# A fused gated-linear-attention and SoLU kernel: weighted keys of the later groups turned by VectorE squares and SBUF transfers in place of array transposes

## The chip, the cores and the metric

The kernel runs on one core of a Trainium2 chip. The metric is the device time of one execution in microseconds (us), as the median of several runs. A core has five engines with their own instruction queues: TensorE (PE in the profile, with its weight loads listed apart as PEld), VectorE (DVE), ScalarE (ACT), GpSimd (POOL) and SyncE (SP). SP issues nearly all DMA transfers here. Each engine works through its queue in program order.

## The reference, cut to what matters

For each of 4 batches and 8 heads of width 48 a state matrix runs over 768 time steps; its output, with the heads side by side, is the input of a layer with a softmax-weighted activation and a layer norm.

```python
for t in range(S):                                     # S = 768, D = 48
    state = alpha[:, :, t, :, None] * state + einsum('bhd,bhe->bhde', k[:, :, t], v[:, :, t])
    y[:, :, t] = einsum('bhd,bhde->bhe', q[:, :, t], state)
x = y.transpose(0, 2, 1, 3).reshape(3072, 384)
h = x @ w_in                                           # 384 -> 1024
solu = h * softmax(h)
ln = (solu - mean(solu)) / sqrt(var(solu) + 1e-6) * g_ln
out = ln @ w_out                                       # 1024 -> 384
```

## The kernel before, in words

Time is cut into six groups of 128 steps (G = 6, P = 128). Within a group the recurrence is written as a masked product: the queries are multiplied by the running products of alpha, the keys by their inverse counterpart (the "weighted keys" kT), and the scores are kT times queries. What came in earlier groups enters through `state`, which is read with the same weighted queries. After a group, `next_state` adds the product of the weighted keys and the values to the state.

**Layout.** A head has 48 features, stored as 32 and 16. The weighted keys `kT` are a tile of 128 x 12 x 128 (features of four batches in four quarters of 32 partitions; twelve blocks j: eight with 32 features of one head each, four with 16 features of two heads each; 128 time steps). `next_state` (L333) needs the same keys with time in the partitions. That is the tile `kg`. `keys_back` (L284) makes it: twelve transposes of 128x128 by PE (L287) into three PSUM banks, and three copies by ScalarE (L289). `next_state` then issues 96 small products (L342), and VectorE adds them to the state (L351).

**Preparing a group.** `keys_T` and `keys`: VectorE transposes of k (L184, L187), then GpSimd's product with the scan (L233). `scan_on` (L216): forward scans of alpha on VectorE. `lasts` (L186) and `firsts` (L183): VectorE transposes of q into `qe` and `qv`. `queries(i)` (L241): GpSimd multiplies them by the scan (L244). `apart` (L235): two ScalarE multiplications (L237) that spread `qe` into the second half of `qv`. `scores` (L262): 64 PE products per half (L268), which read kT and qv. `masked` (L276): VectorE (L279). `read_state` and `read_values`: PE (L300).

**The second part, by group.** `up(g, s)` for s from 0 to 7: six PE products (L366), then e = exp(h) on ScalarE (L380), u = h·e on VectorE (L381), u² on ScalarE (L382). `running(g, s)` (L385) adds e on GpSimd and u² on VectorE to running sums p (both L397). `down(n, half)`: eight PE products for one batch of the group before (L477). `finish(n)` (L482), after both halves: three tiny VectorE operations (L495 to L500), a power on GpSimd (L508), a scaling on ScalarE into `o_sb` (L510), and a store issued by SP (L511).

**The order.** It is written by hand: a manual schedule, in which program order is the order of each queue. The loop from L858 has a round g for each group of the second part, and prepares group g + 1 within it. Each round has eight steps s, and a plan of four tables says what of the preparation goes where: `head` before `up`, `behind` after `up` and after `finish`, `middle` ahead of `down`, `tail` after it. Round 1 uses the plan `first`, round 2 `second`, rounds 3 and 4 `usual`; in round 5 no group is left to prepare. `finish` comes in steps 2, 4 and 6 and after the round.

```python
for s in range(FC):
    at("head", s)
    up(g, s)
    if after is not None:
        finish(after)
    at("behind", s)
    if rise and s:
        running(g, s)
    at("middle", s)
    down(n, half)
    at("tail", s)
```

In `second` the queries are made in step 3, `apart` comes in step 4 and the first scores at the tail of step 5. In `usual` the three stand in steps 2, 3 and 4.

Of the kernel before, what the change touches and what calls it, by code (L numbers as in the profile page):

```python
# [9 lines left out]
FP = mybir.dt.float32  # L10
# [6 lines left out]
P = 128  # L17
# [15 lines left out]
def fast_path(ctx, tc, q, k, v, alpha, moe_w_in, moe_w_out, moe_g_ln, out):  # L33
# [12 lines left out]
    nc = tc.nc  # L46
    B, H, S, D = q.shape
# [5 lines left out]
    NB = H + NP  # L53
# [8 lines left out]
    def pool(name, bufs, **kw):  # L62
        return ctx.enter_context(tc.tile_pool(name=name, bufs=bufs, **kw))

    const = pool("const", 1)
    two = pool("two", 4)
# [32 lines left out]
    TQ = P // 32  # L99
# [21 lines left out]
    kT = const.tile([P, NB, P], FP, name="kT")  # L121
    kg = const.tile([P, NB, P], FP, name="kg")
# [6 lines left out]
    def load(src, dst, g):  # L129
        t = slice(g * P, (g + 1) * P)  # L130
        for b in range(B):
            nc.sync.dma_start(
                out=dst[32 * b : 32 * b + 32].rearrange("t h u d -> t h (u d)"),
                in_=src[b, :, t, :].rearrange("h (t u) d -> t h (u d)", u=TQ),
            )
# [31 lines left out]
    def load_v(g):  # L167
        t = slice(g * P, (g + 1) * P)
        for dst, src in ((slice(0, E0), slice(0, E0)), (slice(48, 64), slice(E0, D))):
            nc.sync.dma_start(  # L170
                out=vn[:, :, :, dst].rearrange("p b h d -> p (b h) d"),
                in_=v[:, :, t, src].rearrange("b h p d -> p (b h) d"),
            )
# [9 lines left out]
    def firsts(src, dst):  # L183
        nc.vector.transpose(out=dst.rearrange("p h (t u) -> p h u t", u=TQ), in_=src[:, :, :, 0:E0])  # L184

    def lasts(src, dst):  # L186
        nc.vector.transpose(  # L187
            out=dst.rearrange("p j (i t u) -> p u j i t", u=TQ, i=2),
            in_=src[:, :, :, E0:D].rearrange("p (j i) u d -> p u j i d", i=2),
        )  # L190

    def alpha_T(g):
        nc.gpsimd.memset(aT[:, :, 0:1], 0.0)
        firsts(an, aT[:, 0:H, 1:SW])
        lasts(an, aT[:, H:NB, 1:SW])
# [20 lines left out]
    def scan_on(g, i):  # L216
        part = slice(NP * i, NP * i + NP)
        s = seed[i % 2]
        if i == 2:
            nc.vector.tensor_copy(out=fend[:, g], in_=h4[:, :, 1])  # L220

        least = small.tile([P, NP, 1], FP, name="least")
        nc.vector.tensor_scalar(out=least, in0=h4[:, part, 1:2], scalar1=LEAST, scalar2=None, op0=ALU.max)  # L223
        nc.vector.reciprocal(out=s[:, :, 0:1], in_=least)
        scan(aT[:, part], aT[:, part], s, False)

    def keys_T(g):
        firsts(kn, kT[:, 0:H])
        lasts(kn, kT[:, H:NB])

    def keys(g):
        for part in (slice(0, H), slice(H, NB)):
            nc.gpsimd.tensor_tensor(out=kT[:, part], in0=kT[:, part], in1=hk[:, part], op=ALU.mult)  # L233

    def apart():  # L235
        for i in range(2):
            nc.scalar.mul(  # L237
                out=qv[:, H : 2 * H].rearrange("p (j i) t -> p j i t", i=2)[:, :, i], in_=qe, mul=parity[:, i : i + 1]
            )

    def queries(i):  # L241
        part = slice(NP * i, NP * i + NP)
        q = qe if i == 2 else qv[:, part]
        nc.gpsimd.tensor_tensor(out=q, in0=q, in1=aT[:, part, 1:SW], op=ALU.mult)  # L244

    def decay(g):

        if g == 0:
            return
        s = state[:, 0:H, 0:64]  # L250
        nc.gpsimd.tensor_tensor(out=s, in0=s, in1=h4[:, 0:H, 1:2].to_broadcast([P, H, 64]), op=ALU.mult)
        for i in range(2):
            s = state[:, H : 2 * H, 0:64].rearrange("p (j i) e -> p j i e", i=2)[:, :, i]
            nc.gpsimd.tensor_tensor(out=s, in0=s, in1=h4[:, H:NB, 1:2].to_broadcast([P, NP, 64]), op=ALU.mult)

    def quarter(b):
        return slice(32 * b, 32 * b + 32)

    def banks(name, shape, n=B):
        return [ps_a.tile([P] + shape, FP, tag=f"a{b}", name=f"{name}{b}") for b in range(n)]  # L260

    def scores(g, half, a=None):  # L262
        a = a or banks("a", [NP, P])
        for i in range(NP):
            h = half * NP + i
            for kb, qb in ((h, h), (H + h // 2, H + h)):
                for b in range(B):
                    nc.tensor.matmul(  # L268
                        a[b][:, i], lhsT=kT[quarter(b), kb], rhs=qv[quarter(b), qb], start=kb == h, stop=kb != h,
                        tile_position=(32 * b, 0), skip_group_check=True,  # L270
                    )
        masks[half] = a
# [11 lines left out]
    def keys_back(g, t=None):  # L284
        t = t or banks("tp", [NP, P], 3)
        for j in range(NB):
            nc.tensor.transpose(out=t[j // NP][:, j % NP], in_=kT[:, j], identity=ident)  # L287
        for i in range(3):
            nc.scalar.copy(out=kg[:, NP * i : NP * i + NP], in_=t[i])  # L289

# [13 lines left out]
    def read_begin():  # L306
        reading["y"] = {}
        reading["begun"] = set()
# [338 lines left out]
    def three(name, where):  # L647
        return [pool.tile([P, NP, P], FP, tag=tag, name=f"{name}{i}") for i, (pool, tag) in enumerate(where)]
# [3 lines left out]
    t = three("tp_a", [(ps_a, "a0"), (ps_a, "a1"), (ps_a, "a2")])  # L652
# [4 lines left out]
    t = three("tp_k", [(ps_a, "a3"), (ps_h, "h"), (ps_h, "h")])  # L657
# [3 lines left out]
    for i in range(3):  # L661
        part = slice(NP * i, NP * i + NP)
        nc.vector.tensor_tensor(out=kT[:, part], in0=t[i], in1=hk[:, part], op=ALU.mult)
    scan_on(0, 0)
    t = three("tp_q", [(ps_o, "o"), (ps_o, "o"), (ps_a, "a0")])
    turned(qn, ends_of(qn), t)
    for i in (2, 0, 1):
        if i == 1:
            scan_on(0, i)
        part = slice(NP * i, NP * i + NP)  # L670
        nc.vector.tensor_tensor(
            out=qe if i == 2 else qv[:, part], in0=t[i], in1=aT[:, part, 1:SW], op=ALU.mult
# [4 lines left out]
    t = [x.tile([P, NP, P], FP, tag=n, name="a_" + n) for x, n in ((ps_h, "h"), (ps_o, "o")) for _ in range(2)]  # L677
# [12 lines left out]
    for f in range(FC):  # L690
        p = 2 + f // 2
# [45 lines left out]
    for i in range(3):  # L737
        scan_back(1, i)
        part = slice(NP * i, NP * i + NP)
# [15 lines left out]
    for i in range(2):  # L755
        scan_on(1, i)
        part = slice(NP * i, NP * i + NP)
# [21 lines left out]
    for i in range(3):  # L779
# [5 lines left out]


    usual = dict(
        head={4: "keys_back", 5: "masked0", 6: "masked1"},
        behind={0: "v keys", 1: "on2 on0 on1", 2: "lasts firsts", 3: "apart", 5: "decay", 6: "alpha", 7: "back"},
        tail={4: "scores0", 5: "scores1", 6: "begin read0 read1", 7: "values"},  # L790
        middle={7: "read2 read3"},
    )
# [1 line left out]
        head={4: "keys_back", 6: "masked0", 7: "masked1"},  # L794
        behind={0: "v keys", 1: "on2 on0", 2: "on1 lasts", 3: "firsts", 4: "apart", 5: "decay", 7: "alpha"},
# [4 lines left out]
        head={4: "keys_back", 6: "masked0", 7: "masked1"},  # L800
        behind={0: "back_late", 1: "v keys", 2: "on2 on0 on1", 3: "lasts firsts", 4: "apart", 5: "decay", 6: "alpha", 7: "back"},
# [4 lines left out]
    def attend(a, what):  # L806

        more = a + 1 < G
        if what == "v":
            load_v(a)  # L810
        elif what == "keys":
            keys_T(a)
            keys(a)
            if more:
                load(k, kn, a + 1)
        elif what[:2] == "on":
            scan_on(a, int(what[2]))
        elif what == "lasts":
            lasts(qn, qe)
            queries(2)  # L820
        elif what == "firsts":
            firsts(qn, qv[:, 0:H])
            queries(0)
            queries(1)
            if more:
                load(q, qn, a + 1)
        elif what == "apart":
            apart()
        elif what == "decay":
            decay(a)  # L830
        elif what == "keys_back":
            keys_back(a)
        elif what[:6] == "scores":
            scores(a, int(what[6]))
        elif what[:6] == "masked":
            masked(int(what[6]))
        elif what == "alpha" and more:
            alpha_T(a + 1)
            alpha_over(a + 1)
            if a + 2 < G:  # L840
                load(alpha, an, a + 2)
        elif what == "back" and more:
            for i in range(3):
                scan_back(a + 1, i)
        elif what == "back_late":
            for i in range(3):
                scan_back(a, i)
        elif what == "begin":
            read_begin()
        elif what[:4] == "read":  # L850
            read_state(int(what[4]))
        elif what == "values":
            read_values(a)
            next_state(a)
# [3 lines left out]
    for g in range(1, G + 1):  # L858
# [10 lines left out]
        for s in range(FC):  # L869
# [14 lines left out]
            if todo:  # L884
                n, half = todo.pop(0)
# [24 lines left out]
    def compare(out, x, bound, op):  # L910
# [6 lines left out]
        out=chunks[:, :, 2], in0=sums[:, :, 2], scalar=0.25, in1=sums[:, :, 3], op0=ALU.mult, op1=ALU.is_le  # L917
# [6 lines left out]
    else:  # L924
# [9 lines left out]
        out=bad, in0=all_ok[0:1, 0:1], scalar1=float(P * ends[-1]), scalar2=None, op0=ALU.is_lt  # L934
# [451 lines left out]
```

## Time and profile before

| | |
|---|---|
| median of 14 runs | 404.93 us (402.73 to 409.52) |
| the profiled execution's own time | 402.58 us |
| its span, first to last instruction | 400.8 us |
| PE busy | 376.5 us, 94% |
| VectorE busy | 256.4 us, 64% |
| ScalarE busy | 146.3 us, 36% |
| GpSimd busy | 118.5 us, 30% |
| key turns by PE (L287), 72 in all | 272 ns each in the records, overlapping |
| copies to kg (L289), 18 in all | 586 ns each |
| rounds 3 and 4 | from about 214 to 272 and from 272 to 330 us |

A line of the timeline gives start and duration in us, the engine, the line of the code, the operation, output and input with their shapes, and a count of merged instructions. In brackets stands the idle time before it and what ended that. PE's records overlap, since its products are pipelined; so the start-to-start distance between one kind of work and the next tells what a block of products takes from PE's stream. The table of stretches gives busy time and instruction count for each engine in the order PE, PEld, DVE, ACT, POOL, then the granted clock, the DMA share and GB/s.

### The profile page before, as it was taken

The numbers are of one execution on the slowest core, as the hardware profiler recorded it, in microseconds if no ns is written. First come the engines' busy times: TensorE is split into PE (matmuls) and PEld (weight loads), VectorE is DVE, ScalarE is ACT, GpSimd is POOL, SyncE is SP. The second block draws the span as 40 slices with busy tenths as digits, with TensorE's granted clock in tenths as the row PEclk, the third lists the DMA queues.
The fourth block names the chain that finished last, engine by engine and source line by source line (L and its number), as shares of the span: only waits on it lengthen the run. The fifth ranks groups of instructions, "written<-read, shape, count | busy, mean of one in ns | idle before, by whom it ended". The sixth has DMA issues, their size and how long they took to land. (4 is left out here: it accounts for less than half of the span.)

```text
span 400.8 us, 11119 instructions
## 1 busy us (share of the span) xinstructions
PE 376.5 (94%) x4929; PEld 229.9 (57%) x4929; DVE 256.4 (64%) x415; ACT 146.3 (36%) x253; POOL 118.5 (30%) x118
## 2 busy tenths in 40 slices
PE   8698999769997798999999999999999999999995
PEld 8685355346743466555657555666556575555552
DVE  0998879996659882897782894674865413444510
ACT  2627773553522543223433143343152132223100
POOL 5020000031014993076510446210475110333200
PEclk9989999999999999999999999999999999999999
DMA  9966988304346305433030921003300000000011
GB/s 184 204 173 179 222 260 139 81 20 100 103 74 105 80 3 108 54 100 79 21 101 20 158 73 51 2 23 69 32 20 21 23 3 21 20 20 12 30 41 47
DMA packets 86409, 30.82 MB, mean 77 GB/s; under 512 B 67912, under 2 KB 84560, under 8 KB 86352
## 3 DMA queue, kind: packets, MB, share of 16 engines
q1 hardware_dynamic: 85328, 29.11, 33.8%
q8 instruction: 40, 0.66, 0.7%
q10 hardware_dynamic: 1024, 0.92, 0.7%
q14 instruction: 17, 0.14, 0.1%
HBM read 25.30 MB, written 4.72 MB: 75 GB/s over the span
## 5 line engine op out<-in xcount | busy, mean ns | idle before, releaser
L366 PE MATMUL h<-x,w_in 128*128 128x512 f32 x288 | 132.4, 600 | 4.7 <-DVE room L381 3.5
L477 PE MATMUL o<-w_out,room 128*128 128x385 f32 x384 | 133.2, 491 | 1.1 <-DVE least L223 1.1
L477 PEld LDWEIGHTS o<-w_out,room 128*128 128x128 f32 x384 | 71.4, 190 | 57.1 <-issue 15.2
L366 PEld LDWEIGHTS h<-x,w_in 128*128 128x128 f32 x288 | 52.6, 189 | 64.1 <-issue 49.4
L381 DVE TENSOR_TENSOR room<-h,e 128x512 f32<-128x512 f32 x40 | 27.5, 688 | 56.8 <-ACT e L380 56.7
L508 POOL TENSOR_TENSOR r<-sums,mhalf 128x1 f32<-128x1 f32 x20 | 12.1, 607 | 167.5 <-DVE sums L500 167.4
L380 ACT ACTIVATE e<-h 128x512 f32<-128x512 f32 x40 | 23.9, 596 | 82.3 <-PE h L366 82.3
L397 POOL TENSOR_TENSOR p<-p,e 128x512 f32<-128x512 f32 x30 | 42.1, 1402 | 21.9 <-ACT e L380 21.7
L382 ACT ACTIVATE u<-room 128x512 f32<-128x512 f32 x40 | 25.2, 630 | 50.1 <-DVE room L381 50.1
L279 DVE TENSOR_TENSOR sT<-a,mask 128x512 f32<-128x512 f32 x44 | 27.2, 679 | 11.1 <-PE a L268 11.1
L268 PE MATMUL a<-qv,kT 32*128 32x128 f32 x704 | 25.8, 288 | 5.8 <-DVE least L223 2.4
L268 PEld LDWEIGHTS a<-qv,kT 32*128 32x128 f32 x704 | 22.9, 195 | 12.8 <-issue 3.7
L397 DVE TENSOR_TENSOR p<-p,u 128x512 f32<-128x512 f32 x30 | 23.9, 797 | 7.0 <-ACT u L382 7.0
L209 DVE TENSOR_TENSOR_SCAN hT<-aT,unit 128x516 f32<-128x516 f32 x18 | 21.9, 1261 | 8.8 <-ACT aT L655 8.7
L209 DVE TENSOR_TENSOR_SCAN aT<-aT,seed 128x516 f32<-128x516 f32 x18 | 25.7, 1426 | 0.6
L351 DVE TENSOR_TENSOR state<-state,kv 128x512 f32<-128x512 f32 x10 | 6.9, 687 | 28.4 <-PE kv L342 28.4
L300 PE MATMUL y<-sT,vn 128*32 128x128 f32 x768 | 23.4, 274 | 1.1 <-issue 0.6
L331 ACT COPY x<-y 128x384 f32<-128x384 f32 x24 | 11.5, 480 | 32.9 <-PE y L300 32.9
L233 POOL TENSOR_TENSOR kT<-kT,hT 128x1024 f32<-128x1024 f32 (+1 forms) x8 | 13.7, 1736 | 31.9 <-DVE kT L184 31.9
L300 PEld LDWEIGHTS y<-sT,vn 128*32 128x32 f32 x768 | 20.9, 110 | 3.7 <-issue 2.8
L300 PE MATMUL y<-qv,state 32*32 32x128 f32 x1280 | 20.1, 278 | 1.9 <-issue 1.5
L300 PEld LDWEIGHTS y<-qv,state 32*32 32x32 f32 x1280 | 15.9, 103 | 9.5 <-issue 6.5
(140 smaller groups left out, 393.5 us busy)
## 6 DMA issues: line engine op xcount, KB each, us to landing
an<-in_alpha_dram SPq DMA_DIRECT2D x20, 192.0 KB, 4.1
out_dram<-o_sb SPq DMA_DIRECT2D x20, 192.0 KB, 1.9
room<-in_moe_w_out_dram SPq DMA_DIRECT2D x8, 384.0 KB, 3.9
kn<-in_k_dram SPq DMA_DIRECT2D x16, 192.0 KB, 4.2
qn<-in_q_dram SPq DMA_DIRECT2D x16, 192.0 KB, 3.4
vn<-in_v_dram SPq DMA_DIRECT2D x5, 512.0 KB, 5.7
room<-in_moe_w_in_dram SPq DMA_DIRECT2D x16, 128.0 KB, 3.9
kn<-in_k_dram SPq DMA_DIRECT2D x4, 384.0 KB, 5.8
```

The lines of the kernel that those rows point to most:

```text
L209: nc.vector.tensor_tensor_scan(out=o, data0=a, data1=s, initial=1.0, op0=ALU.mult, op1=ALU.add)
L233: nc.gpsimd.tensor_tensor(out=kT[:, part], in0=kT[:, part], in1=hk[:, part], op=ALU.mult)
L268: nc.tensor.matmul(a[b][:, i], lhsT=kT[quarter(b), kb], rhs=qv[quarter(b), qb], start=kb == h, stop=kb != h, tile_position=(32 * b, 0), sk ...
L279: nc.vector.tensor_tensor(out=sT[:, b, half * NP : half * NP + NP], in0=a[b], in1=mask[:, None, :].to_broadcast([P, NP, P]), op=ALU.mult,)
L300: nc.tensor.matmul(y_bank(b)[quarter(r), a], lhsT=lhsT, rhs=rhs, start=(b, r) not in begun, stop=stop, tile_position=(row, 32 * r), skip_g ...
L366: nc.tensor.matmul(h, lhsT=w_in[:, a, f * P : (f + 1) * P], rhs=d["x"][:, a].rearrange("p b t -> p (b t)"), start=(a == 0), stop=(a == KC ...
L380: nc.scalar.activation(out=e, in_=h, func=AF.Exp)
L381: nc.vector.tensor_tensor(out=u, in0=h, in1=e, op=ALU.mult)
L382: nc.scalar.activation(out=u2, in_=u, func=AF.Square)
L397: eng.tensor_tensor(out=p, in0=d[0][i] if f == 1 else p, in1=d[f][i], op=ALU.add)
L477: nc.tensor.matmul(d["o"][:, 0 : DM + 1], lhsT=u_of(g, f)[:, b * P : b * P + P], rhs=w_out[:, f], start=(f == 0), stop=(f == FC - 1), skip ...
L508: nc.gpsimd.tensor_tensor(out=r, in0=s[:, 3:4], in1=mhalf, op=ALU.pow)
```

## The change

Two things are edited. A new function `keys_moved` makes `kg` without PE: for each half of the twelve blocks VectorE transposes the 32x32 squares of kT (128 x 768 elements in one instruction) into a buffer of the pool `two`, and 16 DMA transfers on SP's queue each carry 32 partitions x 6 x 32 elements to their place in `kg`. Both halves make 32 transfers. And the plan `usual`, which serves groups 4 and 5, loses `keys_back` at the head of step 4 and gets `moved` behind step 2; `lasts` and `firsts` go from step 2 to step 3, `apart` from step 3 to step 4. The scores stay at the tails of steps 4 and 5. The new branch runs only where a later group follows (`more`), which holds for group 4 and not for group 5. For group 5 neither way of making `kg` runs, and its `next_state` multiplies what is left in `kg`; the state after the last group is not read.

```diff
+    def keys_moved():
+
+        n = NB // 2
+        for half in range(2):
+            part = slice(n * half, n * half + n)
+            t = two.tile([P, n, TQ, 32], FP, tag="two", name="squares")
+            nc.vector.transpose(
+                out=t.rearrange("p j i d -> p (j i d)"), in_=kT[:, part].rearrange("p j t -> p (j t)")
+            )
+            for b in range(B):
+                for i in range(TQ):
+                    nc.sync.dma_start(out=kg[32 * i : 32 * i + 32, part, quarter(b)], in_=t[quarter(b), :, i])
...
     usual = dict(
-        head={4: "keys_back", 5: "masked0", 6: "masked1"},
-        behind={0: "v keys", 1: "on2 on0 on1", 2: "lasts firsts", 3: "apart", 5: "decay", 6: "alpha", 7: "back"},
+        head={5: "masked0", 6: "masked1"},
+        behind={0: "v keys", 1: "on2 on0 on1", 2: "moved", 3: "lasts firsts", 4: "apart", 5: "decay", 6: "alpha", 7: "back"},
         tail={4: "scores0", 5: "scores1", 6: "begin read0 read1", 7: "values"},
         middle={7: "read2 read3"},
     )
...
+        elif what == "moved" and more:
+            keys_moved()
         elif what == "keys_back":
             keys_back(a)
```

## The prediction

> **What bounds the kernel now.** First the page's busy shares and its clock row, then the table of the two stretches that hold the edit: rounds 3 and 4 of the planned loop, which prepare groups 4 and 5.
>
> ```profile
> PE 376.5 (94%) x4929; PEld 229.9 (57%) x4929; DVE 256.4 (64%) x415; ACT 146.3 (36%) x253; POOL 118.5 (30%) x118
> ...
> PEclk9989999999999999999999999999999999999999
> ```
> ```profile
> 214.00:272.00 58.00, 58.00 (x788) 34.99 (x781) 37.85 (x60) 20.23 (x34) 20.95 (x20) 1.00 0.28 56
> 272.00:330.00 58.00, 58.00 (x809) 35.04 (x801) 31.04 (x55) 16.94 (x30) 21.09 (x19) 1.00 0.16 29
> ```
>
> In both stretches PE is busy for all of the 58.00 us. So there is no gap that could absorb anything: each us taken from PE's stream there is won, each us for which PE has to wait is lost. VectorE (37.85 and 31.04), ScalarE and GpSimd have room on average, but they are strict queues, so their order matters.
>
> Third, the timeline of all engines around the keys' turning, in round 3:
>
> ```profile
> 233.02 0.68 DVE L381 TENSOR_TENSOR room<-h,e 128x512 f32<-128x512 f32 x1
> ...
> 234.18 1.11 DVE L187 STREAM_TRANSPOSE qe<-qn 128x512 f32<-128x512 f32 x1
> ...
> 235.13 2.04 DVE L184 STREAM_TRANSPOSE qv<-qn 128x1024 f32<-128x1024 f32 x1
> ...
> 235.69 0.60 ACT L380 ACTIVATE e<-h 128x512 f32<-128x512 f32 x1 [0.29 <-PE h L366]
> ...
> 238.02 1.47 PE L287 MATMUL tp<-ident,kT 128*128 128x128 f32 x12
> ...
> 238.85 1.32 ACT L237 ACTIVATE qv<-qe,parity 128x512 f32<-128x512 f32 x2
> 238.98 1.45 DVE L397 TENSOR_TENSOR p<-p,u 128x512 f32<-128x512 f32 x1 [0.70 <-ACT u L382]
> 239.33 2.74 PE L366 MATMUL h<-x,w_in 128*128 128x512 f32 x6
> ...
> 244.59 2.07 PE L268 MATMUL a<-qv,kT 32*128 32x128 f32 x64
> ...
> 246.59 0.70 PE L366 MATMUL h<-x,w_in 128*128 128x512 f32 x1
> ```
>
> Columns: start, duration, engine, line, operation. The twelve turns hold PE's stream from 238.02 to 239.33, the next start: 1.31 us. The scores (L268) start at 244.59 and run to 246.59. They need the queries, and the last part of those is `apart` (L237), which ends at 240.17: 4.4 us of slack. Round 4 repeats this 57.48 us later (turns 295.50, scores 302.07).
>
> Fourth, and decisive: round 2 already runs in the order that the change brings (queries in step 3, `apart` in step 4), with its scores a step later. Its timeline:
>
> ```profile
> 181.86 1.11 DVE L187 STREAM_TRANSPOSE qe<-qn 128x512 f32<-128x512 f32 x1
> ...
> 182.82 2.09 DVE L184 STREAM_TRANSPOSE qv<-qn 128x1024 f32<-128x1024 f32 x1
> ...
> 184.99 2.62 POOL L244 TENSOR_TENSOR qv<-qv,aT 128x512 f32<-128x512 f32 x2 [0.75 <-DVE qv L184]
> ...
> 187.57 1.78 POOL L397 TENSOR_TENSOR p<-p,e 128x512 f32<-128x512 f32 x1
> ...
> 189.31 0.55 POOL L508 TENSOR_TENSOR r<-sums,mhalf 128x1 f32<-128x1 f32 x1
> ...
> 189.89 0.58 ACT L510 ACTIVATE o_sb<-o,r 128x384 f32<-128x384 f32 x1 [3.20 <-POOL r L508]
> 190.37 1.32 ACT L237 ACTIVATE qv<-qe,parity 128x512 f32<-128x512 f32 x2
> ...
> 190.96 2.18 PE L268 MATMUL a<-qv,kT 32*128 32x128 f32 x64
> ...
> 193.07 0.70 PE L366 MATMUL h<-x,w_in 128*128 128x512 f32 x1
> ```
>
> This is a chain over three queues: the queries' transposes, GpSimd's products, behind them its running sum p, behind that the power r of step 4's `finish`, behind that ScalarE's scaling o_sb, and only then `apart`, in front of which `finish` stands. From the start of `lasts` (181.86) it is 8.51 us to `apart` and 11.21 us to the end of the scores.
>
> **What the Trainium skill says.** "VectorE: DVE Perf Modes", section "The three transpose paths": VectorE turns 32x32 blocks only, TensorE a full 128x128; hence the transfers, which carry the blocks to other partitions. No row here shows the moving. "Vector Engine (DVE) Microarchitecture Reference", section 3.8: a transposition sustains one element per cycle and lane. The trace agrees for dense tiles read from PSUM (128 and 256 elements: 307 and 442 ns, 1.05 ns an element), not for the strided ones (512 and 1024: 1.10 and 2.06 us, 1.88 ns). "SBUF — State Buffer", section "Who interferes with whom": a VectorE instruction with two SBUF inputs and a GpSimd one that reads SBUF exclude each other. The trace agrees: p at 238.98 took 1.45 us instead of 0.69. "TensorE: Matmul & The Clock Gate", section "What's actually happening": an idle window of about 3.4 us halves PE's clock. PE's longest wait here (2.7 us) left no mark in the clock row.
>
> **The change, part by part.**
>
> *Removed.* Twelve turns and three kg copies (1.53 us of ScalarE) in each round: PE −1.31 each, −2.62 us. The copies are worth nothing beyond that: ScalarE next waits for PE (0.50 before e at 242.11). Group 5 gets no turned keys at all, because the new branch asks for a later group; its state product then uses group 4's keys, and nothing reads that state.
>
> *Squares, round 3 only.* Two dense transposes of 128x768. Low end from the PSUM rows: 0.17 + 768 x 1.05 ns = 0.98 us, with the next start 0.16 earlier (as 234.18 + 1.11 against 235.13): 0.82. High end from the strided rows: 1.58, so 1.42. I take the low one, since source and result are dense: 1.64 for both, at most 2.84.
>
> *Queries a step later.* Without the change `lasts` starts at 234.18. Now, in VectorE's queue, L381 of step 3 stands in front of it, and this waits for PE's h through e, which ends at 236.29. So round 4, which has no squares: L381 at 236.32, `lasts` 0.60 later at 236.92. Round 3: squares until 235.82; then p, which waits for GpSimd's p (free now, so it runs from 234.79 to 236.06), until 236.66; L381; `lasts` at 237.26.
>
> *`apart` behind `finish`.* Adding round 2's 11.21 us, the scores end at 248.13 in round 4 (in round 3's times) and 248.47 in round 3. PE without the turns would have started them at 244.59 − 1.31 = 243.28 and ended at 245.28. So PE waits 2.85 and 3.19 us. Against the 246.59 of now that is **+1.54 and +1.88**. Behind the waiting scores on PE stand all later products; what follows (masks, state products) hangs on PE itself and moves along. PE's idle piece is about 2.6 to 3.0 us, as it does the first scores (their queries are ready by 242) before it stops, so I put nothing for the clock.
>
> *The 32 transfers, round 3.* 192 pieces of 128 bytes each. On SP's queue a load of 256 pieces takes 0.45 us, a store of 128 0.36: 0.40 each, 12.8 us from about 235.8, hence to 248.6. The packets: in this stretch 10,976 took 26.7% of 16 engines' 58 us, 22.6 ns each; 6,144 of them are 8.7 us, so issuing is the slower. Landed by about 251; PE wants the keys at 272. Cover 21 us, price 0. Moved past on SP: q's load (wanted a round later) and one store, whose buffer is next needed near 274: 0. GpSimd's queue issues none. PE's waits for the transfers' semaphores: 51 ns each in the trace, none or up to 16; 0 to 0.8, I take 0.3.
>
> *Sum.* 1.54 + 1.88 + 0.30 = **+3.7 us**. The profiled execution took 402.58 (span 400.8 and 1.8 around it), so 406.3; the median of the runs is 404.93, 2.35 higher. Adding the same to the median gives **408.6**. With the high squares (+0.96) and waits (+0.5) it is 410.1; the median of such scattered runs (402.73 to 409.52) is sure to about 1 us, so 407 to 411.3 for this case.
>
> **Rivals.**
>
> A, *faster*: the queries are ready when PE gets to them. Then only −2.62 and the 0.3 of waits remain: 402.6. It takes `lasts` at 243.28 + 2.0 − 11.21 = 234.07 at the latest; the break-even is 235.38. For it speaks the present slack of 4.4 us; against it the wait for PE's h in front (236.29) and round 2. 0.10.
>
> B, *partly hidden*: the chain is shorter than round 2's, where p lost 0.5 us to VectorE (1.78 against 1.27), and `apart` or the first scores overlap more. With 0.5 to 1.2 us less in each round the sum is +1.3 to +2.7: about 407. 0.13.
>
> C, *late transfers*: if each holds SP for 1.55 us (the median of the v loads) the last lands near 235.8 + 49.6 + 1.9 = 287.3, PE waits 13 us at 274 and the time is 422. It decides from 1.15 us each. Against it: pieces are few per transfer. 0.05.
>
> **How the numbers follow.** The likeliest case has 0.72. Half a per cent (2 us) is about what a measurement of this kernel can tell from no change. Faster is A, 0.10; within it B and the likeliest case's low tail, 0.18; slower the rest, 0.72. The range from 405.0 to 411.3 leaves out A and C.
>
> **What would show it.** Right: in rounds 3 and 4 PE waits some 3 us inside L268, released by ScalarE's L237, itself behind L510 and L508; no L287 after round 2; `lasts` after the L381 of step 3. Wrong: L268 without a wait (A), a wait under 2 us (B), or L342 waiting for transfers (C); dense transposes of 1.6 us would put round 3 at +2.8.

## Result, and the profile after

The changed kernel takes 411.81 us (median of 10 runs, 408.93 to 416.86), the kernel before 405.08 (47 runs). The ratio is 1.0177, 95% interval 1.0138 to 1.0217: some 7.2 us slower. The sign and the chain were as predicted; the size was about double.

The profiled execution of the changed kernel was one of its slower ones (416.64 us, span 414.8), as was the second one that is shown further down: its rounds begin 6.75 us late, owing to stages that the change does not touch. So the two traces are compared by round, each counted from the first product of `up(g, 0)` to that of the next round.

| | before | after | difference |
|---|---|---|---|
| round 3 | 57.48 | 61.66 | +4.18 |
| round 4 | 57.48 | 60.61 | +3.13 |
| round 5 and the end | 69.37 | 69.31 | −0.06 |
| sum | | | +7.25 |

That sum agrees with the ratio, so the answer lies in rounds 3 and 4. Lines of the code below L289 stand 13 further down now (L366 is L379, L342 is L355 and so on).

The timeline of round 3 in the changed kernel, to be read beside the one of before:

```profile
240.84 1.83 DVE L297 STREAM_TRANSPOSE squares<-kT 128x768 f32<-128x768 f32 x2
...
243.86 1.11 DVE L187 STREAM_TRANSPOSE qe<-qn 128x512 f32<-128x512 f32 x1
...
246.93 2.63 POOL L244 TENSOR_TENSOR qv<-qv,aT 128x512 f32<-128x512 f32 x2 [0.68 <-DVE qv L184]
...
249.50 1.28 POOL L410 TENSOR_TENSOR p<-p,e 128x512 f32<-128x512 f32 x1
...
250.04 0.50 PE L268 MATMUL a<-qv,kT 32*128 32x128 f32 x8
...
250.88 0.93 POOL L521 TENSOR_TENSOR r<-sums,mhalf 128x1 f32<-128x1 f32 x1
...
251.84 0.58 ACT L523 ACTIVATE o_sb<-o,r 128x384 f32<-128x384 f32 x1 [2.30 <-POOL r L521]
252.32 1.32 ACT L237 ACTIVATE qv<-qe,parity 128x512 f32<-128x512 f32 x2
...
253.08 2.30 PE L268 MATMUL a<-qv,kT 32*128 32x128 f32 x56 [2.54 <-ACT qv L237]
...
255.31 4.19 PE L379 MATMUL h<-x,w_in 128*128 128x512 f32 x6
...
259.34 1.14 PE L490 MATMUL o<-w_out,room 128*128 128x385 f32 x3
```

The predicted chain is there link by link: queries, p, r, o_sb, `apart`, and PE standing 2.54 us within the scores until ScalarE's L237 lets it go. `lasts` starts at 243.86, which is 237.11 in the times of before (predicted 237.26). What was not predicted is the line after the scores: the same six products that took 2.68 us (246.59 to 249.27) now take 4.03 (255.31 to 259.34), although they wait for nothing. In the profile before:

```profile
246.59 2.84 PE L366 MATMUL h<-x,w_in 128*128 128x512 f32 x6
249.27 2.75 PE L477 MATMUL o<-w_out,room 128*128 128x385 f32 x8
```

The table of stretches of the changed kernel shows what goes with it; the third number from the right is the granted clock.

```profile
253.50:254.50 1.00, 1.00 (x40) 0.92 (x37) 0.00 (x0) 0.14 (x1) 1.00 (x2) 1.00 0.15 25
254.70:258.00 3.30, 3.30 (x19) 1.56 (x12) 2.48 (x4) 0.00 (x0) 0.51 (x1) 0.50 0.22 36
258.10:262.00 3.90, 3.90 (x12) 1.86 (x10) 1.07 (x2) 1.23 (x2) 1.27 (x1) 1.00 0.24 38
```

PE resumes at full clock, falls to half some 1.6 us later, and stays there for 3.4 us. Round 4, without squares and transfers, shows the same:

```profile
311.69 0.50 PE L268 MATMUL a<-qv,kT 32*128 32x128 f32 x8
314.56 2.33 PE L268 MATMUL a<-qv,kT 32*128 32x128 f32 x56 [2.36 <-ACT qv L237]
316.82 4.16 PE L379 MATMUL h<-x,w_in 128*128 128x512 f32 x6
320.82 2.75 PE L490 MATMUL o<-w_out,room 128*128 128x385 f32 x8
```

The third piece is the state product of group 4 in round 3, 2.75 us (282.13 to 284.88) instead of 1.88 (272.07 to 273.95). Before and after:

```profile
272.07 1.95 PE L342 MATMUL kv<-vn,kg 128*32 128x64 f32 x96
273.95 2.84 PE L366 MATMUL h<-x,w_in 128*128 128x512 f32 x6
```
```profile
282.13 2.81 PE L355 MATMUL kv<-vn,kg 128*32 128x64 f32 x96
284.88 2.84 PE L379 MATMUL h<-x,w_in 128*128 128x512 f32 x6
```

The record of its line counts the waits that stand as instructions of their own in PE's queue:

```profile
L355 PEldq EVENT_SEMAPHORE  x16: 51/51/51, 281.5 to 283.6; - x16
```

Sixteen of 51 ns are 0.82 us. The data had landed long before: the issues of the 32 transfers end at 264.13, and none took more than 3.1 us from issue to landing.

### The profile page after: what moved, and what is told of

Read it like the earlier page. It is cut to its first block, busy times and chain, and to the rows that moved or that the text cites. A ratio compares the mean times of both kernels' runs of the same rounds, so it can differ in the third digit from the quotient of the medians.

```text
span 414.8 us, 11113 instructions
## 1 busy us (share of the span) xinstructions
PE 382.4 (92%) x4905; PEld 230.0 (55%) x4905; DVE 258.5 (62%) x417; ACT 143.5 (35%) x247; POOL 117.3 (28%) x118
## 5 line engine op out<-in xcount | busy, mean ns | idle before, releaser
L379 PE MATMUL h<-x,w_in 128*128 128x512 f32 x288 | 137.7, 619 | 7.2 <-DVE g_col L609 3.8
L379 PEld LDWEIGHTS h<-x,w_in 128*128 128x128 f32 x288 | 54.6, 196 | 70.1 <-issue 52.9
L410 POOL TENSOR_TENSOR p<-p,e 128x512 f32<-128x512 f32 x30 | 41.1, 1369 | 27.9 <-ACT e L393 27.9
L268 PE MATMUL a<-qv,kT 32*128 32x128 f32 x704 | 27.4, 295 | 10.2 <-ACT qv L237 5.4
L410 DVE TENSOR_TENSOR p<-p,u 128x512 f32<-128x512 f32 x30 | 22.5, 749 | 5.4 <-ACT u L395 5.4
```

Of the source, the lines that this page charges most:

```text
L268: nc.tensor.matmul(a[b][:, i], lhsT=kT[quarter(b), kb], rhs=qv[quarter(b), qb], start=kb == h, stop=kb != h, tile_position=(32 * b, 0), sk ...
L379: nc.tensor.matmul(h, lhsT=w_in[:, a, f * P : (f + 1) * P], rhs=d["x"][:, a].rearrange("p b t -> p (b t)"), start=(a == 0), stop=(a == KC ...
L410: eng.tensor_tensor(out=p, in0=d[0][i] if f == 1 else p, in1=d[f][i], op=ALU.add)
```

## Experiments

**Theory:** PE waits for the late queries behind `finish`, each wait costs a stretch at half clock on top, and the transfers cost only the waits for their semaphores. **Rivals:** squares and transfers are the cost; the queries are late on GpSimd already, whatever stands before `apart`; the slow block has another cause than the clock.

### The shift alone

```diff
-        head={5: "masked0", 6: "masked1"},
+        head={4: "keys_back", 5: "masked0", 6: "masked1"},
-        behind={..., 2: "moved", 3: "lasts firsts", 4: "apart", ...},
+        behind={..., 3: "lasts firsts", 4: "apart", ...},
```

> The plan's shift alone: queries in step 3, `apart` in step 4, and the turns of both rounds stay on PE (no squares, no transfers). Theory (the late queries hold PE, and PE's idle stretch then costs clock): the scores of rounds 3 and 4 end where they ended in round 4 of the changed kernel, 1.82 us later than before in each round, so +3.6 us against the kernel before; PE idles only about 1 us in L268, so the products behind it should run at full clock (2.68 us a block, not 4.0). If a stretch that short costs clock too: +6.3. Rival (the squares and transfers are what costs): within 0.5 us of the kernel before.

Measured: 409.16 us, ratio 1.0109 (1.0042 to 1.0176). Rounds 3 and 4 last 59.33 us each, +1.85 against before (1.82 was expected). PE's timeline in round 3:

```profile
247.08 0.50 PE L268 MATMUL a<-qv,kT 32*128 32x128 f32 x8
248.98 2.01 PE L268 MATMUL a<-qv,kT 32*128 32x128 f32 x56 [1.40 <-ACT qv L237]
250.92 2.84 PE L379 MATMUL h<-x,w_in 128*128 128x512 f32 x6
253.60 2.76 PE L490 MATMUL o<-w_out,room 128*128 128x385 f32 x8
```

With no square and no transfer in it the kernel is slower, so the shift alone is enough to lose time. The turns on PE use up 1.31 us of the wait, and what is left, 1.40 us, is followed by a block of 2.68 us: no clock is lost.

### Queries and `apart` in their old places

```diff
-        behind={..., 2: "moved", 3: "lasts firsts", 4: "apart", ...},
+        behind={..., 2: "lasts firsts", 3: "apart moved", ...},
```

> The changed kernel with queries and `apart` back in steps 2 and 3, and the squares and transfers behind `apart` in step 3. Theory: no wait in L268 and no clock loss; what stays is the turns saved, -1.31 us in each of two rounds, and +0.87 us of waits for the transfers in L355: -1.75 us against the kernel before, about 403.3. Rival (squares and transfers cost): still slower than before by 2 us or more.

Measured: 403.82 us, ratio 0.9967 (0.9930 to 1.0004). By round −0.46 and −1.32, in sum −1.78: as expected, though the ratio alone could not tell it from no change. The wait is gone from rounds 3 and 4; squares and transfers are not what made the kernel slow.

### Only `apart` a step earlier

```diff
-        behind={..., 3: "lasts firsts", 4: "apart", ...},
+        behind={..., 3: "lasts firsts apart", ...},
```

> The changed kernel with only `apart` moved, from step 4 to the end of step 3, so that it stands before `finish` in ScalarE's queue; squares, transfers and queries as in the change. Theory: the wait in L268 falls from 2.5 us to under 0.3 in both rounds, the clock loss goes with it, and the time is -1.75 us (to -1.2) against the kernel before. Rival (the queries on GpSimd are late by themselves): L268 still waits 1 us or more, now for L244, and the time is slower than before.

Measured: 403.34 us, ratio 0.9945 (0.9911 to 0.9979). The timeline of round 3:

```profile
239.25 1.33 ACT L237 ACTIVATE qv<-qe,parity 128x512 f32<-128x512 f32 x2 [1.66 <-POOL qe L244]
239.90 2.63 POOL L244 TENSOR_TENSOR qv<-qv,aT 128x512 f32<-128x512 f32 x2 [0.69 <-DVE qv L184]
...
243.01 2.07 PE L268 MATMUL a<-qv,kT 32*128 32x128 f32 x64
...
243.85 0.93 POOL L521 TENSOR_TENSOR r<-sums,mhalf 128x1 f32<-128x1 f32 x1
```

One word in the plan turns 1.8% slower into 0.5% faster. The queries, still a step late, are done in time (242.53 against 243.01). What held PE was ScalarE's queue: `apart` behind an o_sb that waited for GpSimd. By round it gains 0.09 and 1.31; in round 3 the state product took 3.03 us here instead of 2.75, with the same sixteen waits, for which no experiment gives a cause.

### The wait filled, too much

```diff
+        elif what == "busy":
+            warm(24, ps_a, "a3")
...
-        tail={4: "scores0", ...
+        tail={4: "busy scores0", ...
```

> The changed kernel with 24 idle products of 128x128 (about 2.6 us of PE, their results unused) ahead of the first scores in rounds 3 and 4: they fill the wait and move nothing else. Theory: the scores end where they do in the changed kernel, and the block of products behind them takes 2.68 us instead of 4.0, so 2.7 us less than the changed kernel, +4.6 against the kernel before. Rival (the slow block has another cause, the masks or the transfers beside it): the block still takes 4.0 us and the time stays at +7.2.

Measured: 414.81 us, ratio 1.0248 (1.0177 to 1.0318). A miss in size: the 24 products are 48 records and took 5.45 us, twice the wait, so they delayed the scores themselves. The blocks behind took 2.68 us, though, which favours the clock as their cause.

### The wait filled, to measure

The same with `warm(11, ps_a, "a3")`, and then with `warm(5, ps_a, "a3")`.

> The changed kernel with the wait before the first scores of rounds 3 and 4 filled by 11 idle products (22 records of 0.11 us, 2.5 us of PE, results unused), since 24 took 5.45 us and were too many. Theory (PE's idle stretch costs clock): the scores end where they do in the changed kernel, and the block of six products behind them takes 2.68 us instead of 4.03 and 4.00. Round 3 lasts 60.3 us instead of 61.66 and round 4 59.3 instead of 60.61; against the kernel before +4.6 us. Rival (another cause for the slow block): the block stays at 4.0 us and the rounds at 61.66 and 60.61.

> The changed kernel with 5 idle products (1.1 us of PE, results unused) ahead of the first scores in rounds 3 and 4, which leaves PE idle for about 1.4 us. Theory: so short a stretch costs no clock, as in the kernel with the shift alone; blocks of 2.68 us, rounds of 60.3 and 59.3 us, 2.7 us less than the changed kernel, and no less than with 11. Rival (any wait of PE costs clock): blocks of 4.0 us.

Measured: 11 products 408.32 us, ratio 1.0118 (1.0049 to 1.0187), rounds 60.50 and 58.99; 5 products 408.92 us, ratio 1.0103 (1.0050 to 1.0157), rounds 60.12 and 59.00. PE's timeline with 5:

```profile
245.10 1.28 PE L435 MATMUL warm<-ones 128*128 128x128 f32 x10
246.31 0.61 PE L268 MATMUL a<-qv,kT 32*128 32x128 f32 x8
248.22 2.01 PE L268 MATMUL a<-qv,kT 32*128 32x128 f32 x56 [1.30 <-ACT qv L237]
250.16 2.84 PE L379 MATMUL h<-x,w_in 128*128 128x512 f32 x6
252.84 2.76 PE L490 MATMUL o<-w_out,room 128*128 128x385 f32 x8
```

Useless work makes the kernel some 3 us faster, with squares, transfers and masks as in the change. So the slow block was the clock. The two filled versions were traced once each, but their other runs agree: their lowest are 406.93 and 406.01 us, the lowest of the changed kernel is 408.93. Nor do the losses belong to its two traced executions alone: in none of its 18 runs was the mean clock above 0.991, where the filled versions reached 0.994 and 0.998 and the kernel before 1.000. The version with 5 also measures the wait without it: from the moment at which PE wanted the scores to their end it is 5.06 us in round 3 and 4.92 in round 4 with 5 products (5.27 and 5.13 in the changed kernel), where 2.00 would do; the version with 11 gives 5.07 and 4.91.

### The change once more

> The changed kernel once more, for a second profile. Theory (each of the two waits in L268 is followed by a stretch at half clock): rounds 3 and 4 last 61.7 and 60.6 us again, with blocks of 4.0 us behind the first scores, +7.2 us against the kernel before. If a wait of this length costs clock only by chance, as the 2.65 us wait near 126 us does (seen with and without), one or both blocks take 2.68 us and the rounds 60.3 and 59.3.

Measured: 414.20 us, ratio 1.0224 (1.0176 to 1.0272); rounds 61.45 and 60.42. The stretches after the two waits:

```profile
254.00:257.20 3.20, 3.20 (x57) 2.98 (x57) 0.04 (x1) 0.46 (x1) 2.02 (x3) 0.51 0.27 42
315.50:318.70 3.20, 3.20 (x57) 2.98 (x50) 0.38 (x1) 0.23 (x1) 1.80 (x3) 0.50 0.17 57
```

Again half clock after both, here from the scores on. That makes four losses after four waits in two profiles; how many chances these really are, the last section says.

### The dead work of the last group, left out of the kernel before

```diff
-            next_state(a)
+            if more:
+                next_state(a)
...
-        elif what == "keys_back":
+        elif what == "keys_back" and more:
```

> The kernel before without the turned keys and the state product of the last group, whose state nothing reads; the rest, group 4's turns on PE too, as before. Theory: the part of the change that needs no squares and no transfers is worth the turns' 1.31 us and, beyond the change, the product's 1.88 us, both in round 4: -3.2 us, 0.992 of the kernel before. Rival (PE's time there is covered by something else): less than 1 us.

Measured: 403.45 us, ratio 0.9986 (0.9943 to 1.0029), which proves nothing by itself. By round: 57.48 and 55.07, so −2.41 instead of −3.2. The state product had covered ScalarE's copies of x, for which PE now waits:

```profile
326.43 3.70 PE L300 MATMUL y<-sT,vn 128*32 128x128 f32 x128
330.73 2.84 PE L366 MATMUL h<-x,w_in 128*128 128x512 f32 x6 [0.60 <-ACT x L331]
```

### Sixteen transfers, and the best version

```diff
-            t = two.tile([P, n, TQ, 32], FP, tag="two", name="squares")
+        t = pair.tile([P, NB, TQ, 32], FP, tag="x", name="squares")
...
-                    nc.sync.dma_start(out=kg[32 * i : 32 * i + 32, part, quarter(b)], in_=t[quarter(b), :, i])
+                nc.sync.dma_start(out=kg[32 * i : 32 * i + 32, :, quarter(b)], in_=t[quarter(b), :, i])
```

Both with the old places of queries and `apart`; the second also leaves out the last group's state product.

> The changed kernel with queries and `apart` in their old places and the squares of both halves in one buffer, so that 16 transfers of twelve blocks do what 32 of six did. Theory (L355 waits 51 ns for each of 16 semaphore instructions): eight instructions are left, the product block takes about 2.3 us instead of 2.75, and the time is -2.2 us against the kernel before, 0.4 under the version with 32. Rival (it waits for the data): the block stays at 2.75 us.

> The last version together with the last group's state product left out, which nothing reads. Theory: -2.2 - 1.9 = -4.1 us against the kernel before, 0.990, some 0.9 us under the version that keeps group 4's turns on PE. Rival: the transfers' waits and the squares eat the 1.31 us of group 4, and both are equal.

Measured: sixteen transfers 403.21 us, ratio 0.9951 (0.9915 to 0.9988), rounds 56.42 and 56.17, in sum −2.37. The line of its state product:

```profile
L352 PEldq EVENT_SEMAPHORE  x8: 51/51/51, 270.4 to 271.2; - x8
```

Half the instructions, and the product takes 2.13 us (+0.25 over before) instead of 2.75: the rival, which kept 2.75, is out, and the cost follows the number of transfers waited for. It is not simply 51 ns each: eight fewer are 0.41 us, and 0.62 was saved. (The buffer also changed its pool.) The best version takes 401.06 us, ratio 0.9927 (0.9894 to 0.9960), rounds 56.45 and 55.07: −3.44 us by the traces, faster than both kernels. Of this only 1.03 us comes from turning group 4's keys by squares and transfers; 2.41 us is the work for a state that nothing reads.

## Why the prediction missed

- *Turns removed, −1.31 us a round:* right. From the round's start to the scores PE needs 26.82 and 26.81 us instead of 28.12.
- *Squares, 1.64 us for both:* right, 1.75 by the next start (240.84 to 242.59). That is 1.14 ns an element with the overhead, near the 1.05 ns of the dense tiles that the prediction compared with the Trainium skill ("Vector Engine (DVE) Microarchitecture Reference", section 3.8: one element per cycle and lane).
- *The chain and PE's wait, 3.19 and 2.85 us:* right. With the clock kept up (5 idle products) it is 5.06 − 2.00 = 3.06 and 4.92 − 2.00 = 2.92. Round 2 of the profile before had been the right thing to read.
- ***"So I put nothing for the clock"*: the step that failed.** The changed kernel lost 0.21 us up to the end of the scores (5.27 against 5.06, 5.13 against 4.92) and 1.35 and 1.32 in the block behind them: 3.1 us for both rounds, most of the missing 3.5. The ground was one profile, in which a longest wait of 2.7 us had left no mark, together with the idle window of about 3.4 us that the skill names. One profile cannot show that: the same wait does leave a mark in others (below). And the clock row that the prediction shows does have a mark, the 8 in its third slice: half clock for 3.4 us behind a wait of 2.35 us, shorter than the ones it forecast.

```profile
19.78 3.29 PE L268 MATMUL a<-qv,kT 32*128 32x128 f32 x64 [2.35 <-DVE least L223]
```
```profile
20.39:23.81 3.42, 3.42 (x73) 3.42 (x71) 3.08 (x4) 0.01 (x1) 2.06 (x3) 0.50 0.70 179
```
- *Transfers hidden, cover 21 us:* right in effect, though each held SP for 0.60 us instead of 0.40, so that issuing took 21.5 us instead of 12.8. PE wanted the keys 18 us after the last issue.
- *Waits for the transfers' semaphores, 0.3 of 0 to 0.8 us:* mis-sized, +0.87. All sixteen possible instructions were there, and next to none of their 0.82 us was hidden.
- *The sum.* Turns −2.61, waits without the clock loss +5.98, clock +3.09, semaphores +0.87: +7.33, against +7.25 in the trace and +3.7 predicted. The range had no room for a clock loss.

Rival A's break-even (`lasts` by 235.38) was sound arithmetic with a remedy overlooked: putting `apart` in front of `finish` takes three links out of the chain, and there the change is faster.

## What to carry to other kernels

When a step moves within a hand-written order, list what stands in front of it in each in-order queue it passes, and what those instructions wait for; here one scaling that waited for another engine decided the sign. Price a wait of TensorE of about 1.8 us or more at its length plus a possible stretch at half clock (some 1.5 us each here), even if one profile shows such a wait without it; where it cannot be avoided, fill it until less than that is left. And count the semaphore waits that many small transfers leave in the consumer's queue.

## What the runs showed of the hardware

**The clock is set window by window, and where a wait falls in the windows is chance.** The skill's "TensorE: Matmul & The Clock Gate", section "What's actually happening", has the clock halved after an idle window of about 3.4 us, and calls the window free-running. The twelve profiles (before, after and ten experiments) agree with the windows: the changes of the granted clock within each lie whole multiples of 3.413 us apart, on a grid whose first edge lies anywhere from 0.71 to 3.33 us behind the first instruction. They differ in that a window need not be idle throughout: shorter waits sufficed, and the same wait in untouched code went both ways.

| wait of PE | us | at half clock afterwards |
|---|---|---|
| scores of rounds 3 and 4, partly filled or with the turns kept | 1.16 to 1.40 | 0 of 4 |
| state reads of round 1, no releaser in the profile | 1.26 to 1.83 | 3 of 12, all at 1.81 or 1.83 |
| scores of group 1 | 2.02 | 3 of 12 |
| products of round 1 behind L381 | 2.65 | 5 of 12 |
| scores of rounds 3 and 4, changed kernel | 2.36 to 2.54 | 4 of 4 |

What decides is how much of the idle time falls into one window. The grid, laid over the twelve traces, has 1,384 windows at full clock. All 28 in which PE's products left 2.0 us or more idle were followed by a window at half clock, none of the 1,344 with less than 1.8 us, and 6 of the 12 between. Below is the wait of the table's fourth row in two profiles, before and then the shift alone, as three windows each. The first number behind the comma is PE's busy time, and what it lacks to 3.41 is idle.

```profile
122.79:126.21 3.42, 2.33 (x15) 1.56 (x13) 3.35 (x4) 0.00 (x0) 2.24 (x2) 1.00 0.98 221
126.21:129.62 3.41, 1.84 (x5) 0.89 (x6) 3.34 (x7) 1.11 (x2) 0.00 (x0) 1.00 0.03 7
129.62:133.03 3.41, 2.59 (x7) 1.04 (x6) 3.41 (x4) 1.61 (x4) 2.68 (x2) 1.00 0.00 0
```
```profile
122.68:126.09 3.41, 2.83 (x16) 1.76 (x14) 3.34 (x4) 0.00 (x0) 2.73 (x2) 1.00 0.94 201
126.09:129.50 3.41, 1.34 (x3) 0.68 (x4) 3.34 (x6) 1.11 (x2) 0.00 (x0) 1.00 0.21 40
129.50:132.92 3.42, 3.42 (x5) 1.30 (x4) 3.42 (x5) 1.12 (x3) 2.19 (x2) 0.50 0.01 2
```

In the kernel before, an edge cuts the wait into 1.09 and 1.57 us; in the other, 2.07 us fall into one window, and the next runs at half clock. The changed kernel's first wait:

```profile
251.24:254.65 3.41, 1.57 (x48) 1.50 (x52) 0.16 (x1) 1.80 (x3) 3.41 (x5) 1.00 0.25 40
254.65:258.06 3.41, 3.41 (x20) 1.64 (x17) 2.48 (x4) 0.00 (x0) 0.56 (x1) 0.50 0.23 37
```

Here 1.84 us were idle in the window, near the limit. The second wait falls on the same place of the grid: the two stretches at half clock begin at 254.65 and 316.09, 18 windows apart, and so do those of the other profile (254.07 and 315.51). The four losses are thus closer to two draws than to four. It also explains why PE resumed at full clock: the slow stretch begins at the next edge, not at the end of the wait. That the limit is set by idle time alone, and where exactly it lies, was not tested; it is read from these twelve traces.

The mean clock of a run goes with its time: of 99 runs of before, those at 0.998 or more have a median of 402.8 us, those below 0.985 one of 408.6. So such windows are likely a part of the spread of the runs of before (401.61 to 411.75); how large a part, the runs did not separate.
